# A gather waits for the landing of the third gather ahead instead of the sixth, under a new order

## The chip, the core and the metric

The kernel runs on one core of a Trainium2 chip. Five engines work side by side: TensorE (PE), VectorE (DVE), ScalarE (ACT), GpSimd (POOL) and SyncE (SP); each takes its own instructions in order, and they wait for one another by semaphores. Sixteen DMA engines move data between the chip's memory and the core's buffers. The metric is the device time of one launch in microseconds (us).

## What is computed

The reference adds three things to an input `x` of 2048 rows and 448 columns: `x` itself, a long convolution with gates (A), and a mixture of very many small experts (B). Cut to what matters:

```
xn = layernorm(x)
# A: a 4-tap convolution on k, times v, then a causal convolution of length 2048
#    for each of 448 channels (by Fourier transform), gated by xn
kv  = shift_conv(A_k, A_shift_k) * A_v
y   = irfft(rfft(kv, 4096) * rfft(A_ssm_k, 4096))[:2048] + kv * A_ssm_D
A   = xn * y
# B: 16 heads; each picks 2 of 64*64 experts for each row
q1, q2 = split(xn @ B_w_q)                  # 16 heads, 256 + 256
s1, s2 = q1 @ B_k1.T, q2 @ B_k2.T           # 64 scores each
top two of the sums of the two best of s1 and of s2 -> experts e, weights g = softmax
B   = sum over heads and picks of g * gelu(xn . B_u[e]) * B_v[e]
out = x + A + B
```

For each of the 2048 rows 32 experts are fetched, each a row of `B_u` and a row of `B_v`. In the kernel the two tables lie side by side (`uv`, 896 numbers of 4 bytes for one expert).

## The kernel before, in words

The 2048 rows are 16 tiles `T` of 128. B runs in 128 batches of eight to a tile: batch `b` holds 512 pairs of a row and an expert, and is fetched by four gathers, `r` = 0 to 3. A gather is one indirect DMA that GpSimd issues (line 586): 128 rows of 896 numbers from `uv` into a slot of `ring`, by the list `idx`. The ring holds five batches (`RING`), so the gathers of batch `b` overwrite batch `b - 5`, once its last use is over.

A batch then passes through the engines: VectorE multiplies the four fetched `U` parts by the spread-out rows of xn in one instruction ("prod", line 619); ScalarE sums each of the four parts (line 625) and applies gelu (line 627); GpSimd multiplies by the weights and spreads the coefficients ("co" and "coef", lines 633 and 632; from batch 104 on, `LATE`, VectorE does this); TensorE multiplies the coefficients into the `V` parts and adds up in `pv` ("val", line 638). Around it TensorE makes the scores of later tiles (lines 477 to 481) and the transforms of A (lines 720, 767 and 771, 814, 858 and 865); SP loads A's inputs (`kvh`, line 348, 400 KB each), the Fourier matrices and the query weights.

Nothing of this order is found at run time. A planner in Python (`Plan`) walks through all steps with a cost for each, keeps a clock for each engine and one for the DMA, and lets the ready step with the lowest key go first. A key is the step's due time plus an offset from the table `RANK`: for each group of steps a few knots, between which the offset is interpolated along the group. The order in which the planner starts the steps is the order in which each engine's instructions are written out. In the planner a gather occupies POOL for 0.96, its landing occupies the DMA for `DLAND` = 1.2, and a step on another engine that needs it waits 0.15 and 1.6 more for the two hops.

Two things hold a gather back beside its ring slot and its list. The first is its mark: the last step on PE that ended at least `LEAD` = 0.5 before the gather's start in the plan; on the chip the gather waits for that instruction. The second is the landing of an earlier gather, `OUTSTANDING` places ahead, both in the plan (`after`) and on the chip:

```python
if len(gins) >= OUTSTANDING:
    tc.add_manual_dep(g, gins[-OUTSTANDING], ..., reason="gathers on their way")
...
after = (landed[-OUTSTANDING],) if len(landed) >= OUTSTANDING else ()
i = op("POOL", 0.96, f, r=[("idx", T % 8, j // 2)], w=rk, key=tb(b) - 14.0, after=after, name="gather")
d = op("DMA", DLAND, None, key=tb(b) - 14.0, after=(i,), name="landing")
...
elif o.pace:
    tc.add_manual_dep(i, o.pace.last, ..., reason="gathers keep pace with PE")
```

After some val steps a few small matmuls fill a short planned idle time of PE (line 1094); how many is worked out from the plan.

Of the kernel before, what the change touches and what calls it, by code (L numbers as in the profile page):

```python
# [18 lines left out]
S, D, H, E = 2048, 448, 16, 64  # L19
# [75 lines left out]
class Plan:  # L95
# [13 lines left out]
    def op(self, eng, dur, fn, r=(), w=(), key=0.0, acq=None, rel=None, nb=0.0, name="", after=()):  # L109
        o = Op()  # L110
        o.eng, o.dur, o.fn, o.key, o.acq, o.rel, o.nb, o.name = eng, dur, fn, key, acq, rel, nb, name
        o.deps, o.users, o.start, o.pace, o.last = set(after), [], None, None, None
        o.group = name + self.stage
        for k in r:
            if k in self.writer:
                o.deps.add(self.writer[k])
            self.readers.setdefault(k, []).append(o)
        for k in w:
            if k in self.writer:
                o.deps.add(self.writer[k])  # L120
            o.deps.update(self.readers.get(k, ()))
            self.writer[k] = o
            self.readers[k] = []
        o.deps.discard(o)
        self.ops.append(o)
        return o
# [90 lines left out]
CONV = {"in0": (77.8, 157.8), "sp0": (177.4, 373.1), "out0": (383.1, 393.1),  # L217
        "in1": (388.1, 396.9), "sp1": (396.9, 561.6), "out1": (561.6, 586.6)}
DMA_RATE = 0.421
OUTSTANDING = 6  # L220
LEAD = 0.5
RANK = {
# [6 lines left out]
    "SPlate@out1": (-46.5, -46.5, -46.5, -57.0), "SPwq": (0.0, 0.0, 45.5, 0.0), "SPx": (6.0, 6.0, 19.5, 22.0), "bad": (178.0, 100.0, 62.0, 46.5),  # L229
    "co": (-1740.0, 1197.0, -1227.0, -3082.0), "coef": (-33.5, -40.5, -46.0, 6.0), "ds": (22.0, -93.0, -157.5, -36.0),  # L230
    "es": (79.5, 106.0, 108.5, 109.0), "fin@out0": (-413.0, -296.5, -286.5, 40.5), "fin@out1": (0.5, -32.0, -27.5, -27.5),
    "flag": (-22.5, -47.5, -14.0, -53.0), "fold": (50.0, 36.5, 0.0, 0.0), "gat": (13.0, 13.0, 13.0, 9.0), "gate@out1": (6.5, 14.5, -60.5, -123.0),
    "gateG@out0": (83.0, -13.0, 54.5, 64.0), "gateG@out1": (-81.0, -64.5, -137.5, -144.0), "gather": (2080.5, 2339.0, 2195.5, 3324.0),
    "gelu": (164.5, 57.0, 133.0, 285.5), "hh@sp0": (8.0, -21.0, -25.0, -24.5), "hh@sp1": (123.5, 413.0, 124.0, 164.0),
    "idx": (-94.5, -44.0, 35.5, -83.0), "join": (-75.5, -75.5, -75.0, -66.0), "kv@in0": (-829.5, -476.5, -686.5, -690.5),
    "kv@in1": (85.0, 90.5, 112.5, 143.0), "landing": (36.0, 242.5, 1246.5, -266.5), "late@out1": (87.0, -40.5, -164.0, -260.0),
    "lateD@out1": (344.5, 342.0, 247.0, 196.0), "mi": (-280.5, -150.0, 455.5, 455.5), "mx": (-7077.5, -8642.5, -7977.0, -6331.5),
    "newton": (67.5, 142.0, 224.5, 283.5), "pk": (-14.5, -10.0, -32.0, -8.0), "place": (-628.5, -829.0, -301.5, -212.5),
# [6 lines left out]
    "stats": (1206.5, 960.0, 979.0, 837.5), "store": (43.0, 28.0, 12.5, 7.0), "storeD": (23.5, 22.0, 74.0, 52.5),  # L245
# [3 lines left out]
    "tw@sp1": (-23.5, -160.0, -53.5, -133.5), "val": (87.5, -236.5, 21.0, -42.0), "whi": (495.0, 545.0, 210.5, 67.0),  # L249
# [4 lines left out]
}  # L254
LATE = 104
DLAND = 1.2
# [17 lines left out]
def one_pass(ctx, tc, x, wq, kk, uv, kvh, cst1, cst2, fq, out, flag):  # L274
# [119 lines left out]
    def tb(b):  # L394
        return T0 + PACE * min(b, TURN) + PACE2 * max(b - TURN, 0)
# [177 lines left out]
    def last_val(i, b):  # L573

        tc.declare_no_dep(i, group=GROUP, reason="the last product of the batch, which ends after the others, is waited for")
        if b >= 0:
            tc.add_manual_dep(i, vins[b], mybir.DependencyInfo(mybir.DependencyClass.Sync, mybir.DependencyReason.DATA),
                              reason="the products of the batch that was here have been made")

    def gather(T, j):  # L580
        b = NB * T + j
        for r in range(4):
            dst = ring[:, b % RING, r, :]

            def f(r=r, dst=dst):
                g = nc.gpsimd.indirect_dma_start(dst, None, uv, bass.IndirectOffsetOnAxis(ap=idx[:, T % 8, r, j:j + 1], axis=0)).ins  # L586
                last_val(g, b - RING)
                if len(gins) >= OUTSTANDING:

                    tc.add_manual_dep(g, gins[-OUTSTANDING], mybir.DependencyInfo(mybir.DependencyClass.Sync, mybir.DependencyReason.DATA),  # L590
                                      reason="gathers on their way")
# [3 lines left out]
            rk = [("U", b % RING, r), ("V", b % RING, r)]  # L595
            after = (landed[-OUTSTANDING],) if len(landed) >= OUTSTANDING else ()
            i = op("POOL", 0.96, f, r=[("idx", T % 8, j // 2)], w=rk, key=tb(b) - 14.0, after=after, name="gather")
# [559 lines left out]
```

## Time and profile before

| what | value |
|---|---|
| time, median of 3 runs | 909.22 us (908.57 to 912.37) |
| the profiled execution's own time | 899.54 us |
| its span, first to last instruction | 897.6 us |
| its mean granted TensorE clock | 0.931 |
| busy: PE, DVE, POOL, ACT | 734.1, 673.5, 593.5, 568.2 us |
| moved by DMA | 279.47 MB, 311 GB/s on the mean |
| of it by gathers | 234.91 MB |
| gathers (line 586) | 512, first start 41.6 us, last start 871.5 us |
| POOL busy with gathers | 509.3 us, idle just before them 270.6 us |

The rows of the profile that are shown below are of a few views. The page gives busy times, the span in 40 equal slices (a digit is the busy share in tenths), the DMA queues (q0 holds the gathers, q1 the loads and stores issued by SP), and the chain of work that ended last. A group's row has the line, engine, operation, output and input, count, then busy time and mean ns of one, then the idle time just before and what ended it. A row of waits has who waited, for whom, and the us in total, the times and the longest. A row of the timeline has start, duration, engine, line and operation, and in brackets the idle time before it with what ended it; a row of the chain has start, duration and what. A row of stretches has the bounds and the length, the busy time of PE, PE's weight loads, DVE, ACT and POOL with counts, the granted clock, the DMA share and GB/s.

### The profile page before, as it was taken

To read this page: it belongs to the slowest core of one execution; us is meant where nothing else is said; L and a number is where in the kernel's file an instruction comes from. 1 tells how busy PE (TensorE), PEld (TensorE's weight loads), DVE (VectorE), ACT (ScalarE), POOL (GpSimd) and SP (SyncE) were. 2 spreads that over 40 slices of the span, in tenths; PEclk is the share of its full clock that TensorE was granted. 3 is DMA by queue.
4 is the path that set the end of the run, shared out by engine and by line. 5 is a ranking of instruction groups with operands and counts; after the bars stand their busy time and mean duration, and the time that the engine had idled before them with its cause. 6 is when DMAs were issued, how large, how long until landed. Compare 5 with 4: busy or idle time off the path is not lost.

```text
span 897.6 us, 15165 instructions
## 1 busy us (share of the span) xinstructions
PE 734.1 (82%) x4696; PEld 465.9 (52%) x4696; DVE 673.5 (75%) x1570; ACT 568.2 (63%) x1874; POOL 593.5 (66%) x740
## 2 busy tenths in 40 slices
PE   5988988898888889888797878787688887778776
PEld 2436756556555565556465645465343443345554
DVE  3568988887787878787887867758798897864454
ACT  2598664557565766566663675537798887764562
POOL 0157587886777767776777677757877776665550
PEclk9899999998999989998998989999999999997797
DMA  9898798888989999898889899988999999999885
GB/s 372 345 398 296 229 309 304 294 284 301 313 314 318 304 314 311 309 332 297 297 293 344 294 309 343 356 326 295 354 318 325 319 328 313 309 309 336 299 299 143
DMA packets 62586, 279.47 MB, mean 311 GB/s; under 512 B 14112, under 2 KB 23584, under 8 KB 62240
## 3 DMA queue, kind: packets, MB, share of 16 engines
q0 software_dynamic: 40960, 234.91, 75.2%
q1 hardware_dynamic: 21536, 43.49, 13.7%
q8 instruction: 39, 0.64, 0.3%
q14 instruction: 51, 0.42, 0.1%
HBM read 272.29 MB, written 6.08 MB: 310 GB/s over the span
## 4 chain that ended last, share of the span: by engine, by line
PE 49%; ACT 12%; issue 12%; DVE 9%; DMA 7%; POOL 7%; another core or an unknown queue 3%; DVEq 0%; POOLq 0%; SPq 0%; ACTq 0%
PE pv L638 9%; ACT ring L625 6%; POOL ring L586 5%; PE bank L477 4%; PE bank L720 4%; PE bank L478 3%; PE bank L479 3%; PE bank L814 3%; PE pv L1094 3%; PE bank L771 3%; DMA ring<-in_uv_dram,idx 3%; PE bank L865 2%; DVE ring L619 2%; DMA S<-in_kvh_dram 2%
## 5 line engine op out<-in xcount | busy, mean ns | idle before, releaser
L586 POOL DMA_INDIRECT ring<-in_uv_dram,idx x512 | 509.3, 995 | 270.6 <-issue 91.3
L625 ACT ACTIVATE ring<-ring 128x448 f32<-128x448 f32 x512 | 288.4, 567 | 49.8 <-DVE ring L619 30.5
L619 DVE TENSOR_TENSOR ring<-ring,xs 128x1792 f32<-128x1792 f32 x128 | 256.9, 2014 | 54.7 <-DMA ring<-in_uv_dram,idx 37.6
L638 PE MATMUL pv<-ring,cc 128*32 128x448 f32 x1024 | 136.4, 604 | 67.3 <-issue 36.5
L486 DVE MAX8 SC<-bank 128x8 f32<-128x64 f32 x512 | 118.5, 232 | 37.2 <-PE bank L481 10.0
L625 ACT ACTIVATION_READ_ACCUMULATOR ring<-ring 128x1 f32 x512 | 97.0, 189 | 0.0
L1094 PEld LDWEIGHTS pv<-c 128*128 128x128 f32 x596 | 80.3, 201 | 26.6 <-issue 25.5
L477 PE MATMUL bank<-WR,xh 128*128 128x512 f32 x192 | 84.4, 440 | 2.7 <-ACT R L724 1.0
L720 PE MATMUL bank<-c,S 128*64 128x132 f32 x896 | 68.1, 295 | 22.1 <-issue 7.0
L1094 PE MATMUL pv<-c 128*128 128x64 f32 x596 | 85.6, 285 | 0.0
L478 PE MATMUL bank<-WR,xh 128*128 128x512 f32 x192 | 78.1, 407 | 0.0
L638 PEld LDWEIGHTS pv<-ring,cc 128*32 128x32 f32 x1024 | 21.3, 112 | 108.3 <-issue 65.0
L479 PE MATMUL bank<-WR,xl 128*128 128x512 f32 x192 | 77.3, 403 | 0.0
L720 PEld LDWEIGHTS bank<-c,S 128*64 128x64 f32 x896 | 53.1, 143 | 45.3 <-issue 12.5
L771 PE MATMUL bank<-x1b,S 128*128 128x336 f32 x132 | 51.6, 505 | 10.8 <-DVE x1b L839 7.0
L724 ACT ACTIVATE x1b<-bank 128x264 f32<-128x264 f32 x84 | 30.8, 387 | 40.0 <-PE bank L720 29.7
L788 DVE TENSOR_TENSOR S<-bank,S 128x224 f32<-128x224 f32 (+1 forms) x66 | 40.5, 620 | 18.6 <-ACT S L782 13.4
L703 DVE TENSOR_TENSOR S<-S 128x1024 f32<-128x1024 f32 x28 | 34.9, 1245 | 25.7 <-PE bank L720 11.5
L493 DVE FIND_INDEX8 SC<-SC,bank 128x8 uint32<-128x256 f32 x128 | 52.5, 423 | 0.0
L477 PEld LDWEIGHTS bank<-WR,xh 128*128 128x128 f32 x192 | 37.9, 197 | 26.6 <-issue 11.5
L782 ACT ACTIVATE S<-bank 64x112 f32<-64x112 f32 x132 | 33.9, 257 | 21.8 <-PE bank L767 13.0
L632 POOL TENSOR_TENSOR cc<-sm,c 128x128 f32<-128x128 f32 x104 | 46.0, 442 | 2.2
(142 smaller groups left out, 1090.8 us busy)
## 6 DMA issues: line engine op xcount, KB each, us to landing
R<-in_wq_dram SPq DMA_DIRECT2D x16, 896.0 KB
S<-in_kvh_dram SPq DMA_DIRECT2D x28, 400.0 KB
ring<-in_uv_dram,idx POOLq DMA_INDIRECT x512
S<-in_fq_dram SPq DMA_DIRECT2D x32, 128.0 KB
XA<-in_x_dram SPq DMA_DIRECT2D x2, 1344.0 KB
out_dram<-fo SPq DMA_DIRECT2D x12, 224.0 KB
x1b<-out_dram SPq DMA_DIRECT2D x9, 224.0 KB
out_dram<-XA SPq DMA_DIRECT2D x2, 840.0 KB
```

Source lines behind the costliest of these rows:

```text
L477: nc.tensor.matmul(o, xh[:, c, :], wh[:, c, ns], start=(c == 0), stop=False)
L478: nc.tensor.matmul(o, xh[:, c, :], wl[:, c, ns], start=False, stop=False)
L479: nc.tensor.matmul(o, xl[:, c, :], wh[:, c, ns], start=False, stop=False)
L486: nc.vector.max(mx[:, 8 * n + j, :] if safe else m2[:, m, 2 * j:2 * j + 8], bank[s.i][:, 64 * j:64 * j + 64])
L493: nc.vector.max_index(m4i[:, 2 * m + g, :], m2[:, m, 8 * g:8 * g + 8], bank[s.i][:, 256 * g:256 * g + 256])
L586: g = nc.gpsimd.indirect_dma_start(dst, None, uv, bass.IndirectOffsetOnAxis(ap=idx[:, T % 8, r, j:j + 1], axis=0)).ins
L619: op("DVE", dve(m * D), lambda: nc.vector.tensor_mul(U[:, :m, :], U[:, :m, :], xs[:, :m, :D]), r=["xs"], w=u[:m], key=k, name="prod")
L625: op("ACT", 0.575, lambda r=r: nc.scalar.activation(U[:, r, :], U[:, r, :], AF.Copy, accum_out=aw[:, r:r + 1]), w=[u[r], ("aw", b % 4, r)] ...
L638: v = nc.tensor.matmul(pv[32 * r:32 * r + 32, :D], cc[b % 3][:, r, :], ring[:, b % RING, r, D:], start=(j == 0), stop=(j == NB - 1), tile_ ...
L720: nc.tensor.matmul(o[64 * i:64 * i + 64, w * j:w * j + w], src, f1[:, i, :], start=True, stop=True, tile_position=(0, 64 * i))
L771: op("PE", 0.95 * n / 448 + 0.05, lambda t=t, sl=sl: nc.tensor.matmul(bank[sl.i][:, :n], fm, x1[p][:, :, q, t, :], start=True, stop=True), ...
L1094: nc.tensor.matmul(pv[:, D:], ident, c1[:, P:P + 512 - D], start=False, stop=False)
```

## The change

`OUTSTANDING` goes from 6 to 3, so that a gather waits, beside its mark, for the landing of the third gather ahead of it, in the plan and on the chip. The offsets in `RANK` are replaced throughout by ones searched under that limit; each group now has seven knots where it had four, and the group "gate@out0", which had no offset, has one. Nothing else differs: the same steps, planner, costs, `LEAD`, `RING` and due times. Since the order follows from the offsets, every engine's instructions may stand in another order, and the marks, the issues of loads on SP and the filling matmuls may move with it.

```diff
-OUTSTANDING = 6
+OUTSTANDING = 3
 LEAD = 0.5
 RANK = {
-    "DMAc1": (-1.0, 0.0, 8.0, 64.5), "DMAc2": (43.5, 4.0, 37.0, 128.5), "DMAfb@out1": (247.5, -85.5, 210.0, 115.5),
...
-    "gateG@out0": (83.0, -13.0, 54.5, 64.0), "gateG@out1": (-81.0, -64.5, -137.5, -144.0), "gather": (2080.5, 2339.0, 2195.5, 3324.0),
...
+    "DMAc1": (-0.5, 60.0, -4.0, 62.0, 66.0, 88.5, 101.0), "DMAc2": (9.5, -29.0, -37.0, -37.5, -25.5, -32.5, 50.5),
...
+    "gate@out0": (-119.5, -124.5, -110.5, -54.5, -104.0, 5.0, -21.0), "gate@out1": (93.0, 111.0, 62.0, 76.5, 97.5, 44.0, 22.5),
+    "gateG@out0": (-34.0, 21.5, -6.0, -6.0, -4.0, -9.0, -35.0), "gateG@out1": (52.0, 66.5, 99.5, 120.5, 75.0, 42.5, 14.0),
+    "gather": (2662.0, 2607.5, 2615.5, 2445.5, 2351.0, 2680.5, 3398.5), "gelu": (170.0, 120.5, 81.5, 118.5, 162.5, 259.0, 378.0),
...
```

More of the change, by code (lines that the diff above doesn't have):

```diff
@@ L219 @@
 DMA_RATE = 0.421
-OUTSTANDING = 6
+OUTSTANDING = 3
 LEAD = 0.5
 RANK = {
[6 rows of a table removed]
[L229 to L232, printed above, removed]
-    "gateG@out0": (83.0, -13.0, 54.5, 64.0), "gateG@out1": (-81.0, -64.5, -137.5, -144.0), "gather": (2080.5, 2339.0, 2195.5, 3324.0),
[L234 to L238, printed above, removed]
[6 rows of a table removed]
-    "stats": (1206.5, 960.0, 979.0, 837.5), "store": (43.0, 28.0, 12.5, 7.0), "storeD": (23.5, 22.0, 74.0, 52.5),
[3 rows of a table removed]
-    "tw@sp1": (-23.5, -160.0, -53.5, -133.5), "val": (87.5, -236.5, 21.0, -42.0), "whi": (495.0, 545.0, 210.5, 67.0),
[4 rows of a table removed]
[4 rows of a table added]
+    "DMAwq": (-21.5, -19.5, 33.0, -42.5, -89.5, -48.5, 1.0), "DMAx": (-285.0, -148.5, -33.5, 30.5, 52.0, 31.5, -17.5),
[5 rows of a table added]
+    "SPwq": (-14.0, -14.0, -14.0, -13.0, 18.5, -13.0, -4.5), "SPx": (-18.5, -21.0, -21.0, -35.0, -31.0, -14.0, 54.5),
[4 rows of a table added]
+    "fold": (-108.5, -170.5, -136.5, -130.0, -183.0, -187.0, -161.0), "gat": (73.5, 9.5, 30.0, 42.5, 53.0, 173.5, -3.0),
+    "gate@out0": (-119.5, -124.5, -110.5, -54.5, -104.0, 5.0, -21.0), "gate@out1": (93.0, 111.0, 62.0, 76.5, 97.5, 44.0, 22.5),
+    "gateG@out0": (-34.0, 21.5, -6.0, -6.0, -4.0, -9.0, -35.0), "gateG@out1": (52.0, 66.5, 99.5, 120.5, 75.0, 42.5, 14.0),
+    "gather": (2662.0, 2607.5, 2615.5, 2445.5, 2351.0, 2680.5, 3398.5), "gelu": (170.0, 120.5, 81.5, 118.5, 162.5, 259.0, 378.0),
+    "hh@sp0": (-2.0, 38.0, 37.0, 10.0, 10.5, -10.0, -9.0), "hh@sp1": (40.0, 410.5, 385.5, 224.0, 224.5, 217.5, 316.5),
+    "idx": (-458.0, -374.0, -360.5, -370.5, -241.0, -306.5, -364.0), "join": (10.5, 10.5, 10.5, 0.0, 21.5, 10.5, 6.5),
[14 rows of a table added]
+    "spread": (-336.0, -148.5, 25.0, -176.0, -279.0, -123.0, 116.0), "stats": (1255.5, 1039.0, 915.5, 925.0, 934.5, 817.5, 776.5),
+    "store": (-76.5, -136.0, -134.5, -128.0, -206.0, -104.5, -102.0), "storeD": (-6.0, 24.5, -5.5, -15.0, -2.0, 7.5, 75.0),
[5 rows of a table added]
+    "val": (101.5, -42.5, -220.5, -40.0, 50.0, 45.5, -17.0), "whi": (113.5, 207.5, 262.0, 53.5, -97.5, -120.5, -277.5),
[6 rows of a table added]
```

55 rows, old and new, of the table RANK are left out of this document.

## The prediction

> **What bounds the kernel now.** I read the page first, its engine shares, the 40 slices and the DMA queues, then the chain, then the groups and waits of GpSimd, then single stretches of the timeline, because the change concerns one kind of instruction only.
>
> ```profile
> PE 734.1 (82%) x4696; PEld 465.9 (52%) x4696; DVE 673.5 (75%) x1570; ACT 568.2 (63%) x1874; POOL 593.5 (66%) x740
> ...
> DMA  9898798888989999898889899988999999999885
> ...
> q0 software_dynamic: 40960, 234.91, 75.2%
> q1 hardware_dynamic: 21536, 43.49, 13.7%
> ...
> PE 49%; ACT 12%; issue 12%; DVE 9%; DMA 7%; POOL 7%; another core or an unknown queue 3%; DVEq 0%; POOLq 0%; SPq 0%; ACTq 0%
> ...
> L586 POOL DMA_INDIRECT ring<-in_uv_dram,idx x512 | 509.3, 995 | 270.6 <-issue 91.3
> ```
>
> No engine is full. The chain of work that ended last lies on PE for half of its length and changes hands all the time. What is almost full is the transfer side: the DMA row stands at 8 or 9 tenths in nearly every slice, and the gathers' queue (q0) alone takes 75.2% of 16 engines, so a gather costs 0.752 x 897.6 / 512 = 1.32 us of all engines together, and q1's traffic adds 0.137 x 897.6 / 512 = 0.24 us to each. The gathers are therefore a second stream beside PE, and its speed matters.
>
> ```profile
> L586 POOL DMA_INDIRECT ring<-in_uv_dram,idx x512: 943/951/1939, 41.6 to 871.5; - x171
> ...
> L586 POOL DMA_INDIRECT ring<-in_uv_dram,idx x64 | 63.4, 990 | 20.3 <-issue 11.6 <-PE bank L771 6.1 <-remote 1.2
> ...
> 640.00:735.00 95.00, 79.24 (x354) 37.21 (x354) 82.49 (x101) 82.58 (x248) 74.15 (x98) 0.96 0.93 322
> ```
>
> The first row (the answer on the gather's line) says that 512 gathers start within 871.5 - 41.6 = 829.9 us, one every 1.62 us. The other two are the densest stretch, 640 to 735 us: 64 gathers in 95 us, one every 1.48 us. GpSimd's groups there name what ended the idle time before the gathers: its own issue and a mark on PE (L771), no landing. So today the limit of six is not what paces them; the marks and the issue are.
>
> **The change, part by part.** It moves one wait and it re-orders. No instruction is added to any engine: 512 gathers, 128 products, the same coefficients, the same loads.
>
> *The wait.* What matters is how long a gather takes from its start to the moment at which a waiting engine gets going. Three places show it, since there a product on VectorE (line 619) waited for the last gather of its batch. Of each, the gathers before it, and then the product:
>
> ```profile
> 123.70 0.96 POOL L586 DMA_INDIRECT ring<-in_uv_dram,idx  x1 [0.16 <-issue]
> ...
> 125.58 1.13 POOL L586 DMA_INDIRECT ring<-in_uv_dram,idx  x1 [0.16 <-issue]
> 127.02 0.95 POOL L586 DMA_INDIRECT ring<-in_uv_dram,idx  x1 [0.30 <-issue]
> ...
> 128.36 0.96 POOL L586 DMA_INDIRECT ring<-in_uv_dram,idx  x1 [0.15 <-issue]
> ...
> 129.91 0.99 POOL L586 DMA_INDIRECT ring<-in_uv_dram,idx  x1 [0.16 <-issue]
> ...
> 136.09 2.02 DVE L619 TENSOR_TENSOR ring<-ring,xs 128x1792 f32<-128x1792 f32 x1 [1.74 <-DMA ring<-in_uv_dram,idx]
> ```
>
> ```profile
> 700.56 1.17 POOL L586 DMA_INDIRECT ring<-in_uv_dram,idx  x1 [1.01 <-PE bank L771]
> ...
> 702.12 0.96 POOL L586 DMA_INDIRECT ring<-in_uv_dram,idx  x1 [0.15 <-issue]
> 703.09 0.42 POOL L632 TENSOR_TENSOR cc<-sm,c 128x128 f32<-128x128 f32 x1
> 703.67 0.99 POOL L586 DMA_INDIRECT ring<-in_uv_dram,idx  x1 [0.16 <-issue]
> 704.96 0.95 POOL L586 DMA_INDIRECT ring<-in_uv_dram,idx  x1 [0.30 <-issue]
> ...
> 705.94 2.02 DVE L619 TENSOR_TENSOR ring<-ring,xs 128x1792 f32<-128x1792 f32 x1 [1.17 <-DMA ring<-in_uv_dram,idx]
> ```
>
> ```profile
> 867.96 0.95 POOL L586 DMA_INDIRECT ring<-in_uv_dram,idx  x1 [0.30 <-issue]
> 871.52 0.95 POOL L586 DMA_INDIRECT ring<-in_uv_dram,idx  x1 [2.61 <-ACT S L860]
> ...
> 876.15 2.02 DVE L619 TENSOR_TENSOR ring<-ring,xs 128x1792 f32<-128x1792 f32 x1 [3.62 <-DMA ring<-in_uv_dram,idx]
> ```
>
> From start to release: 136.09 - 129.91 = 6.18 us behind a tight row of gathers; 705.94 - 700.56 = 5.38 us in the dense stretch; 876.15 - 871.52 = 4.63 us for the very last gather, which left 3.56 us behind the one before it. The second fence shows the new wait at work by hand: the gather at 704.96 is the third after the one at 700.56, whose release is seen at 705.94. Under the limit it would start about 1.0 us later, and the one behind it would in turn wait for the gather of 702.12.
>
> Under the change gather i cannot start before gather i-3 is released, so three gathers fill one such time: the stream can do no better than a gather per 4.63 / 3 = 1.54 us, 5.38 / 3 = 1.79 us, or 6.18 / 3 = 2.06 us. Against that stand 1.62 us on the average and 1.48 us in the dense stretch, where 5.38 / 1.48 = 3.6 gathers are under way at a time. So by the trace the limit of three lies right at the speed that the kernel needs, while the limit of six (5.38 / 6 = 0.90 us) lies below the spacing that GpSimd's own work allows (703.67 to 704.96 to 706.21, about 1.25 us).
>
> Which value? With three at most, fewer gathers queue ahead than in the dense stretch, so 5.38 us is too long; but two others are nearly always under way, which the gather of 871.52 did not have, so 4.63 us is too short. I take the middle, 5.0 us, a gather per 1.67 us: 512 x 1.67 = 855 us for the stream against 829.9, that is +25 us. At the ends: 512 x 1.54 = 788 us, no loss on the average and only 64 x (1.54 - 1.48) = 4 us in the dense stretch; 512 x 1.79 = 916 us, +87 us. I count the whole of the +25, because the stream has hardly a cover: the products wait for landings already (21 times, 37.6 us, in the row below), and PE's val matmuls (line 638) run in a written order behind them. Early batches have some lead over their products, which can swallow a late gather or two but not a stream that is slower throughout.
>
> The Trainium skill, page "DMA: Bandwidth & Descriptors", section "Anatomy of one DMA — SWDGE (gpsimd) path", speaks against this forecast: it gives a fit of about 2.0 us and the bytes at 436 GB/s for a transfer issued by GpSimd. By that page a gather (234.91 MB / 512 = 0.459 MB) would be an estimated 3.05 us, 4.0 us with its issue, or 1.33 us per gather with three under way, and the limit would cost nothing. The 4.63 and 5.38 us of this trace disagree with it; they were taken with other transfers running.
>
> *What is queued behind the waiting gather.* GpSimd also makes the coefficients of 104 batches (lines 632, 633), in order with the gathers, and PE waits for them:
>
> ```profile
> DVE ring L619 <- DMA ring<-in_uv_dram,idx: 37.6, 21, 4.1
> ...
> PEld pv L638 <- POOL cc L632: 34.0, 26, 2.9
> ...
> PE pv L638 <- POOL cc L632: 25.0, 22, 2.5
> ```
>
> Those are 48 waits and 59 us. A gather that stands 1.67 - 1.25 = 0.42 us longer than its shortest spacing delays a coefficient behind it by as much: at most 48 x 0.42 = 20 us, if every one of these waits still ends last. I take zero, because it is the same pause of GpSimd, already counted in the stream, and keep the 20 us for the upper end.
>
> *The other queues.* The loads on SP are moved by the new order too. Three of them stand on the chain:
>
> ```profile
> 477.51 6.96 DMA S<-in_kvh_dram
> ...
> 593.37 5.64 DMA S<-in_kvh_dram
> ...
> 623.57 6.78 DMA S<-in_kvh_dram
> ```
>
> They share the 16 engines with the gathers. If a shallower queue brought all to the shortest of them, it would give (6.96 - 5.64) + (6.78 - 5.64) = 2.5 us; below nothing, if they are issued later in the new order. I take zero. The same skill page, section "Queues, rings and completion order", says that an engine takes turns between its queues packet by packet; by that a load on SP would not wait behind all gathers that are under way, and the depth would matter little to it. No row here separates the two.
>
> *The new order.* Nothing in the trace of before shows it. Its planner holds a landing for 0.96 + 0.15 + 1.2 + 1.6 = 3.91 us from start to release (the gather's own duration, the two hops, DLAND), so under three it can plan a gather per 1.30 us, where the rows above say 1.54 to 1.79. The order is thus searched for a stream that the chip won't give, and it cannot raise that stream. Where it helps is in moving gathers to places with room. Below, it could take back at most the 37.6 us of VectorE's waits; above, it could cost the 20 us named. I take zero.
>
> *The sum.* 899.5 us (the profiled execution; span 897.6) + 25 = 924.5 us. The median shown, 909.2, lies 9.7 us above that execution, so the forecast for the median is 934 us.
>
> **The rivals.**
> 1. *The limit is hidden.* With fewer under way the transfer falls to 4.6 us, and 1.54 us per gather is enough. For it: the last gather's 4.63 us, and GpSimd idle for 270.6 us before gathers. Against it: two others are under way in a full stream, and the DMA row stands at 8 or 9 tenths even where the gathers are one per 1.62 us. It gives 909 + 0 to 4 us. The fit of the Trainium skill's page "DMA: Bandwidth & Descriptors", above, would make this rival the likeliest.
> 2. *Faster, by the same mechanism from the other side.* Even spacing takes away the bunches: the gather of 129.91 took 6.18 us since it left behind four others within 6.2 us. If such ones came down to 5 us, the products would get back a part of their 37.6 us; a third is 12.5 us, with the loads' 2.5 us 15 us, and 894 us. It decides as soon as a gather's time falls below 3 x 1.62 = 4.86 us, since then the stream has room and only the gain is left. Against it: those 37.6 us stand at 21 places, 4.1 us at most, and the same products would now wait for gathers that start later.
> 3. *Dearer.* The time doesn't fall at all: 1.79 us per gather, 909 + 87 = 996 us. For it: the 0.24 us of q1's traffic stays whatever the depth. Against it: fewer gathers must queue less.
>
> **How the numbers follow.** My forecast, a stream of 1.64 to 1.72 us per gather with its coefficients (918 to 958 us): 0.49. Rival 3: 0.13. Rival 1: 0.13. Rival 2, with a better order as another way to the same sign: 0.25. A change within 0.5% (4.5 us) is what this measurement can't tell from none. So slower 0.62, same 0.13, faster 0.25. The range leaves out half of rival 3 and a good part of rival 2's tail: 893 to 980 us.
>
> **What would show it.** Right: in GpSimd's waits the landing of a gather (DMA ring) becomes a large releaser of the gather, tens of us where the page of before has almost none; the dense stretch thins to about 57 gathers in 95 us (one per 1.67); from a gather's start to the product that it releases it takes about 5.0 us; the DMA row falls by a tenth in places; VectorE's wait for landings grows above 37.6 us. Wrong: gathers still one per 1.5 us in the dense stretch, or releases within 4.6 us, or GpSimd's waits ended by marks on PE as now; then the limit rarely binds and the order decides. If the chain's PE share rises and the span falls, rival 2 holds.

## The result: slower by about a fifth, and the profile after

The changed kernel takes 1075.66 us (median of 4 runs, 1072.58 to 1078.19) against 908.89 us for the kernel before: a ratio of 1.189, 95% interval 1.183 to 1.195, taken from the fast runs (the two medians alone give 1.183). The forecast had the sign and a loop of three gathers as the mechanism, 934 us, and a range up to 980 us; the loss is 167 us instead of 25.

The page of the changed kernel answers line by line to the one of before (shares and counts as there):

```profile
PE 830.9 (77%) x4844; PEld 536.7 (50%) x4844; DVE 675.4 (63%) x1570; ACT 574.7 (53%) x1874; POOL 580.8 (54%) x740
...
DMA  9987767778788888878788888788887787878786
...
q0 software_dynamic: 40960, 234.91, 69.0%
q1 hardware_dynamic: 21536, 43.49, 11.4%
...
DMA 38%; PE 27%; issue 12%; POOL 10%; DVE 10%; ACT 2%; DVEq 0%; POOLq 0%; SPq 0%; ACTq 0%
...
L604 POOL DMA_INDIRECT ring<-in_uv_dram,idx x512 | 497.2, 971 | 466.9 <-DMA ring<-in_uv_dram,idx 142.5
```

Read the chain first: DMA has gone from 7% to 38% of it, PE from 49% to 27%. The gathers' own instructions (now line 604) are no longer than before; what has grown is GpSimd's idle time ahead of them, from 270.6 to 466.9 us, with a landing as the largest releaser. The DMA row has fallen by one or two tenths in 26 of its 40 slices: the transfers have room, and the kernel waits for them all the same.

The gathers' line gives the whole loss in one row (durations in ns, then first and last start):

```profile
L604 POOL DMA_INDIRECT ring<-in_uv_dram,idx x512: 940/946/1971, 39.1 to 1056.7; - x171
```

From first to last gather 1017.6 us pass, 829.9 before: +187.7 us, of which the span shows 1076.1 - 897.6 = +178.5, since the ends around the stream got 9 us shorter. A gather starts every 1.99 us. Who waits for the stream is in the waits (total us, times, longest):

```profile
DVE ring L637 <- DMA ring<-in_uv_dram,idx: 225.4, 74, 6.6
ACT ring L643 <- DVE ring L637: 197.1, 73, 9.2
PEld pv L656 <- POOL cc L650: 153.5, 71, 6.4
POOL ring L604 <- DMA ring<-in_uv_dram,idx: 142.5, 114, 3.8
...
PE pv L656 <- POOL cc L650: 127.6, 58, 6.2
```

Product, sums, coefficients: each step of a batch now stands behind the landing.

Why 1.99 us? A stretch of GpSimd's timeline in the changed kernel (start, duration, in brackets the idle time before) and the chain through the same stretch:

```profile
370.39 0.94 POOL L604 DMA_INDIRECT ring<-in_uv_dram,idx  x1 [1.03 <-PE bank L832]
372.18 0.94 POOL L604 DMA_INDIRECT ring<-in_uv_dram,idx  x1 [0.84 <-PE pv L656]
373.88 0.94 POOL L604 DMA_INDIRECT ring<-in_uv_dram,idx  x1 [0.76 <-issue]
375.64 0.94 POOL L604 DMA_INDIRECT ring<-in_uv_dram,idx  x1 [0.81 <-DMA ring<-in_uv_dram,idx]
377.74 0.95 POOL L604 DMA_INDIRECT ring<-in_uv_dram,idx  x1 [1.15 <-DMA ring<-in_uv_dram,idx]
379.99 0.95 POOL L604 DMA_INDIRECT ring<-in_uv_dram,idx  x1 [1.31 <-DMA ring<-in_uv_dram,idx]
```

```profile
370.39 5.00 DMA ring<-in_uv_dram,idx
375.38 0.26 issue
375.64 5.04 DMA ring<-in_uv_dram,idx
380.68 0.03 issue
380.71 0.05 DVEq L637
380.76 0.04 issue
380.81 2.02 DVE ring L637
```

The fourth gather is the third after the first: 375.64 - 370.39 = 5.25 us for three. The next two loops are 377.74 - 372.18 = 5.56 and 379.99 - 373.88 = 6.11 us; over all 512 it is 3 x 1.99 = 5.97 us. The second view splits the first of these loops: 5.00 us until the landing, 0.26 us until the waiting gather starts. That is the good case. The chain some 35 us later has the other:

```profile
410.76 0.02 POOLq L604
410.77 0.72 issue
411.50 5.24 DMA ring<-in_uv_dram,idx
```

Here a gather has two waits, and one of them stands on an instruction of its own in GpSimd's queue (POOLq). When that one ends last, 0.72 us more pass before the gather starts. The packet records of q0 (80 to a gather, the last 16 of them of 4 bytes) give the averages: 4.64 us from a gather's start to the end of its last packet, 1.35 us from there to the start of the gather that waits for it, which is called the restart below. The semaphore tells of a landing some 0.35 us behind the last packet (the median of the 256 gathers for which the old order under the same wait, the first experiment below, has all the events), so 1.35 us is about 1.0 us behind the landing.

The same records show that most gathers start close behind the landing, far more often than the rows name it: 68% of the gathers start within 1.3 us of the last packet of the third gather ahead, and 91% within 2 us; in the kernel before, 1% start within 2 us of that of the sixth. And the restart is not the price of a wait alone. In 290 of the 509 loops GpSimd had not yet ended the instruction ahead, mostly a gather or a coefficient, when the landing came (put at 0.35 us behind the last packet); there the restart is 1.50 us on the average, in the others 1.15 us.

### The profile page after: what moved, and what is told of

Its sections match the earlier page's. It is cut to its first block, busy times and chain, and to the rows that moved or that the text cites. A ratio compares the mean times of both kernels' runs of the same rounds, so it can differ in the third digit from the quotient of the medians.

```text
span 1076.1 us, 15472 instructions
## 1 busy us (share of the span) xinstructions
PE 830.9 (77%) x4844; PEld 536.7 (50%) x4844; DVE 675.4 (63%) x1570; ACT 574.7 (53%) x1874; POOL 580.8 (54%) x740
## 4 chain that ended last, share of the span: by engine, by line
DMA 38%; PE 27%; issue 12%; POOL 10%; DVE 10%; ACT 2%; DVEq 0%; POOLq 0%; SPq 0%; ACTq 0%
DMA ring<-in_uv_dram,idx 38%; POOL ring L604 7%; PE pv L656 6%; DVE ring L637 4%; PE pv L1112 3%; PE bank L738 2%; PE bank L495 2%; DVE SC L504 2%; PE bank L497 2%; POOL cc L650 2%; PE bank L496 2%; ACT ring L643 2%; PE bank L433 1%; PE bank L789 1%; PE bank L834 1%
## 5 line engine op out<-in xcount | busy, mean ns | idle before, releaser
L604 POOL DMA_INDIRECT ring<-in_uv_dram,idx x512 | 497.2, 971 | 466.9 <-DMA ring<-in_uv_dram,idx 142.5
L637 DVE TENSOR_TENSOR ring<-ring,xs 128x1792 f32<-128x1792 f32 x128 | 257.8, 2016 | 230.7 <-DMA ring<-in_uv_dram,idx 225.4
L656 PE MATMUL pv<-ring,cc 128*32 128x448 f32 x1024 | 155.8, 687 | 164.8 <-POOL cc L650 127.6
L1112 PEld LDWEIGHTS pv<-c 128*128 128x128 f32 x744 | 117.8, 236 | 40.5 <-issue 39.1
L656 PEld LDWEIGHTS pv<-ring,cc 128*32 128x32 f32 x1024 | 22.2, 119 | 209.3 <-POOL cc L650 153.5
L1112 PE MATMUL pv<-c 128*128 128x64 f32 x744 | 123.4, 320 | 0.0
L738 PE MATMUL bank<-c,S 128*64 128x132 f32 x896 | 80.3, 339 | 23.1 <-ACT ring L643 10.9
L495 PE MATMUL bank<-WR,xh 128*128 128x512 f32 x192 | 85.8, 447 | 3.3 <-DVE S L806 1.1
L738 PEld LDWEIGHTS bank<-c,S 128*64 128x64 f32 x896 | 66.0, 170 | 42.7 <-ACT ring L643 15.2
L496 PE MATMUL bank<-WR,xh 128*128 128x512 f32 x192 | 79.1, 412 | 0.0
L650 POOL TENSOR_TENSOR cc<-sm,c 128x128 f32<-128x128 f32 x104 | 46.1, 443 | 5.4
L789 PEld LDWEIGHTS bank<-x1b,S 128*128 128x128 f32 x132 | 26.0, 218 | 41.6 <-DVE S L806 12.1
```

What stands on the lines that cost most here:

```text
L495: nc.tensor.matmul(o, xh[:, c, :], wh[:, c, ns], start=(c == 0), stop=False)
L496: nc.tensor.matmul(o, xh[:, c, :], wl[:, c, ns], start=False, stop=False)
L637: op("DVE", dve(m * D), lambda: nc.vector.tensor_mul(U[:, :m, :], U[:, :m, :], xs[:, :m, :D]), r=["xs"], w=u[:m], key=k, name="prod")
L650: last_val(ve.tensor_mul(cc[b % 3], co[:, :, None].broadcast_to([P, 4, 32]), rep[:, None, :].broadcast_to([P, 4, 32])).ins, b - 3)
L656: v = nc.tensor.matmul(pv[32 * r:32 * r + 32, :D], cc[b % 3][:, r, :], ring[:, b % RING, r, D:], start=(j == 0), stop=(j == NB - 1), tile_ ...
L738: nc.tensor.matmul(o[64 * i:64 * i + 64, w * j:w * j + w], src, f1[:, i, :], start=True, stop=True, tile_position=(0, 64 * i))
```

## The experiments

In all of them `OUTSTANDING` in the plan stays as it was in the kernel named, so order and fill are those of that kernel, and its marks too where they are not said to be left out. Where the wait on the chip is another, it has a number of its own:

```diff
+WAIT = 3
...
-                if len(gins) >= OUTSTANDING:
-                    tc.add_manual_dep(g, gins[-OUTSTANDING], ...)
+                if len(gins) >= WAIT:
+                    tc.add_manual_dep(g, gins[-WAIT], ...)
```

The experiments ran in three groups, each on another chip. The kernel before took 847.43 us in the first, 894.97 in the second and 845.86 in the third, so each ratio is against the kernel before of its own group.

**Wait and order apart (first group).** The old order with the wait for the third:

> The order, the plan and the marks of before; only the wait on the chip is for the third gather ahead. Theory A (the wait alone: a gather per 1.99 us as in the changed kernel, since 4.64 us from start to landing and 1.35 us from landing to the start of the gather that waits make 5.98 us for three): 1050 to 1090 us, first to last gather about 1000 us. Rival B (the new order is what costs, since it was searched for a gather per 1.30 us): at most 990 us. My own prediction's term (1.67 us per gather) would give 934 us.

Measured: 1076.3 us, ratio 1.274 (1.261 to 1.287). The new order with the wait for the sixth (`WAIT = 6`):

> The order, the plan and the marks of the changed kernel; only the wait on the chip is for the sixth gather ahead again. Theory A: the order is near neutral, 895 to 925 us, and the clock that PE is granted comes back to about 0.93 by itself. Rival B: 980 us or more. Rival C (order and wait work on each other: the order suffers only under the wait): 895 to 925 us here, and below 1050 us in the run with the old order and the wait for the third.

Measured: 892.63 us, ratio 1.051 (1.036 to 1.065). The wait alone does all of it, and rivals B and C are out: the old order under the new wait takes the same 1076 us as the changed kernel. But the order is not neutral either: by itself it costs 5.1%, which was not expected. Under the wait for the third nothing of that shows. The two streams, old order first:

```profile
L587 POOL DMA_INDIRECT ring<-in_uv_dram,idx x512: 940/947/1959, 41.5 to 1052.8; - x171
```

```profile
L605 POOL DMA_INDIRECT ring<-in_uv_dram,idx x512: 941/949/1926, 39.1 to 872.3; - x171
...
DVE ring L638 <- DMA ring<-in_uv_dram,idx: 115.7, 57, 5.1
```

That is a gather per 1.98 us, and per 1.63 us with the wait back at six.

**Other depths.** The old order with the wait for the fourth, then the new one:

> The order of before, the wait on the chip for the fourth gather ahead. Theory A: with four in the same loop of about 4.9 + 1.35 = 6.25 us a gather per 1.56 us is possible, below the 1.62 us of before, so only dense stretches lose: 905 to 930 us. If instead every wait for a landing costs by itself, whatever the depth: above 950 us.

> The order of the changed kernel, the wait on the chip for the fourth gather ahead. Theory A: 900 to 935 us, within 10 us of the run with the old order and the wait for the fourth. Rival B: 980 us or more.

Measured: 933.16 us (1.105, 1.094 to 1.116) and 936.63 us (1.110, 1.099 to 1.121). Both lie a little above the expected range, since four gathers took 6.78 us (below) and not the 6.25 us assumed. And the loss of 86 and 89 us is not small: the kernel before is faster on this chip than the 909 us from which the range was drawn. That the two orders agree again, though they differ by 5% under the wait for the sixth, says once more that the loop sets the end. The fifth, in the second group:

> The order of before, the wait for the fifth gather ahead. Theory A: five in a loop of 5.1 + 1.35 = 6.5 us would allow a gather per 1.30 us, near GpSimd's own 1.25 us, so the wait hardly ever ends last: within 15 us of the kernel before. If each wait for a landing costs by itself: half of the loss with the fourth, some 40 us or more.

Measured: 903.05 us (1.008, 1.004 to 1.011), as theory A had it; a wait for a landing doesn't cost by itself. The second, in the third group:

> The order of before, the wait for the second gather ahead. Theory A: start to landing about 4.4 us (one other under way) and 1.35 us from landing to the next start, 5.75 us for two, a gather per 2.88 us, 511 x 2.88 = 1470 us from first to last, 1520 to 1560 us in all. If the time from start to landing falls in proportion to the depth: below 1300 us.

Measured: 1382.78 us (1.633, 1.625 to 1.641), between the two expectations. The stream of the fourth, the fifth and the second, in that order:

```profile
L587 POOL DMA_INDIRECT ring<-in_uv_dram,idx x512: 941/949/1865, 40.6 to 906.9; - x171
```

```profile
L587 POOL DMA_INDIRECT ring<-in_uv_dram,idx x512: 940/947/2022, 41.3 to 875.0; - x171
```

```profile
L587 POOL DMA_INDIRECT ring<-in_uv_dram,idx x512: 940/947/1982, 42.1 to 1355.2; - x171
...
POOL ring L587 <- DMA ring<-in_uv_dram,idx: 406.8, 290, 5.8
```

Divided by 511 these are 1.70, 1.63 and 2.57 us per gather. Times the depth, the loop is 5.14 us at two, 5.94 at three, 6.78 at four; at five (8.2) it no longer binds. By the packet records the time from start to last packet is 4.06, 4.64 and 5.00 us at two, three and four, and the restart 1.08, 1.30 and 1.78 us. At four the landing mostly comes before it is the gather's turn: in 457 of 508 loops GpSimd had not yet ended the instruction ahead, against 287 of 509 at three and 42 of 510 at two. The 1.70 us per gather at four are thus set by GpSimd's own work as well as by the wait. My expectation for two took the restart of three, and counted the 0.35 us from the last packet to the landing twice: the medians from start to landing, the last number of these two rows of DMA issues, are 4.2 us at two and 4.9 us at three (the latter from the changed kernel in the next experiment).

```profile
ring<-in_uv_dram,idx POOLq DMA_INDIRECT x512, 4.2
```

```profile
ring<-in_uv_dram,idx POOLq DMA_INDIRECT x512, 4.9
```

So the transfer does get shorter with fewer under way, but by 0.4 to 0.6 us for each gather less, while the loop loses a whole gather.

The Trainium skill, page "DMA: Bandwidth & Descriptors", section "Anatomy of one DMA — SWDGE (gpsimd) path", gives the fit from which the prediction estimated 4.0 us with the issue. At a depth of two the 4.2 us from start to landing are near it; at three, 4.9 us, they no longer are.

**The whole on one more chip.** The changed kernel in the third group:

> The changed kernel once more, beside the others of this group on one chip. Theory A (a loop of fixed times, three gathers in 5.98 us, sets the end): 1070 to 1080 us whatever the kernel before takes on this chip (847 to 909 us so far), as the old order under the same wait took 1076 us. If PE's clock or the chip's transfer speed sets it: the time moves with that of the kernel before.

Measured: 1074.98 us, ratio 1.269 (1.262 to 1.275). The medians of the kernel before lie up to 63 us apart between groups, those of the changed one 1 us: a stream bound by this loop doesn't use what a chip has to spare. What it is that a chip has to spare was not found.

**The restart.** The marks left out of the changed kernel:

```diff
-            elif o.pace:
+            elif o.pace and o.name != 'gather':
```

> The changed kernel with the marks on PE left out; a gather then waits for the third gather's landing, its ring slot and its list alone. Theory A1 (where a gather has two waits the landing is put on an instruction of its own ahead of the gather, and 0.72 us pass from the end of that one to the gather's start; with one wait the gather itself waits and starts at once): the loop shortens by about 0.5 us in most cases, 5.98 to about 5.45 us, a gather per 1.82 us, 985 to 1010 us. Rival A2 (0.72 us is what GpSimd needs to start a gather after any wait for a landing): 1060 to 1080 us.

Measured: 1052.84 us (1.177, 1.170 to 1.184), where the changed kernel took 1075 us in its own groups: about 22 us less, where 65 to 90 were expected. The waits on their own instruction fell from the first of these rows to the second (the changed kernel's, then this one's):

```profile
L604 POOLq EVENT_SEMAPHORE  x431: 17/17/1397, 48.6 to 1055.3; - x144
```

```profile
L604 POOL DMA_INDIRECT ring<-in_uv_dram,idx x512: 943/949/1943, 39.5 to 1028.1; - x171
L604 POOLq EVENT_SEMAPHORE  x181: 17/43/43, 57.8 to 1026.7; - x181
```

The loop shortened only from 5.97 to 5.80 us. 181 gathers still have a second wait, for their list or ring slot, and in 252 of the 509 loops GpSimd was still on the instruction ahead when the landing came, so that a quicker start after a wait had less to gain there. A1's direction is right (the marks do cost time beside the landing), its size was too large. Then a memset in front of each gather, to take the wait for the landing off it:

```diff
+                if len(gins) >= OUTSTANDING:
+                    c = nc.gpsimd.memset(sm[:, 60:61], 0.0).ins
+                    tc.add_manual_dep(c, gins[-OUTSTANDING], ...)
                 g = nc.gpsimd.indirect_dma_start(...)
```

> The changed kernel; a memset of one column on GpSimd ahead of each gather takes the wait for the landing, the gather keeps its mark. A1: the memset starts at once and the gather about 0.15 us behind it, so that 0.72 us becomes about 0.3 us, the loop about 5.6 us, a gather per 1.86 us, 1000 to 1040 us; the memsets' own time (some 0.2 us each) lies inside the wait. A2: 1060 us or more.

Measured: 1087.85 us (1.215, 1.208 to 1.222), no gain. The timeline of GpSimd shows why, after a wait and without one:

```profile
407.65 0.10 POOL L605 MEMSET sm<- 128x1 f32 x1 [1.02 <-DMA ring<-in_uv_dram,idx]
408.33 0.94 POOL L608 DMA_INDIRECT ring<-in_uv_dram,idx  x1 [0.59 <-DVE SC L504]
...
411.18 0.10 POOL L605 MEMSET sm<- 128x1 f32 x1
411.42 0.98 POOL L608 DMA_INDIRECT ring<-in_uv_dram,idx  x1
```

From the end of a memset that had waited to the gather 0.58 us pass, from one that had not, 0.14 us. Over the whole trace, where the gather is the next instruction, the median is 0.59 us behind the 155 memsets that waited for a landing (90% of them between 0.59 and 0.61) and 0.20 us behind the 261 that waited for nothing. So whatever waits ahead of the gather, the gather starts late behind it; only a gather that does the waiting itself starts soon. A1, which blamed the separate instruction alone, falls in this form, and A2 does as well, because of the 0.26 us above. What GpSimd does in that half microsecond stays open.

**The order's own cost.** The kernel before again, for its profile on the second chip:

> The kernel before once more, for its profile on the chip of these runs, where it takes 847 us instead of 909. All theories: a gather per 1.5 to 1.55 us. If the two chips differ in the gathers' time from start to landing, it is below 5 us in the dense stretch here; if they differ in the clock that PE is granted, it is above 0.94.

Measured: 890.57 us in one run; a gather per 1.61 us, a clock of 0.922. That chip is near the one of the first result, so why the other two run this kernel in 846 and 847 us was not settled. Its wait of VectorE for landings is 36.2 us, against the 115.7 us of the new order above, which ran on another chip:

```profile
DVE ring L619 <- DMA ring<-in_uv_dram,idx: 36.2, 24, 3.3
```

The new order without its marks, under the wait for the sixth, and the old one without its marks, both in the third group:

> The order of the changed kernel, the wait for the sixth, the marks on PE left out. Theory O1 (what the new order costs under the wait for the sixth, 5.1%, comes from marks that let the gathers start too late: they start 9.4 us behind the release of their ring slot on the median where the old order has 5.0 to 5.5, and VectorE waits 115.7 us for landings instead of 36.2): within 2% of the kernel before, VectorE's waits for landings below 70 us. Theory O2 (the sequence of the steps itself costs it): 4% or more above the kernel before.

> The kernel before without its marks on PE. If marks only delay gathers: 1 to 3% faster. If they keep the queue short and GpSimd's coefficients in time: up to 3% slower, with more than the sixth under way never possible. No theory of the wait for the third gather hangs on it; it is the other half of the run without marks in the new order.

Measured: 859.3 us (1.013, 1.008 to 1.019) and 838.23 us (0.988, 0.982 to 0.994).

```profile
L605 POOL DMA_INDIRECT ring<-in_uv_dram,idx x512: 940/947/1999, 40.8 to 839.7; - x171
...
DVE ring L638 <- DMA ring<-in_uv_dram,idx: 85.6, 46, 4.2
```

```profile
L586 POOL DMA_INDIRECT ring<-in_uv_dram,idx x512: 940/949/1949, 41.5 to 813.2; - x171
...
DVE ring L619 <- DMA ring<-in_uv_dram,idx: 40.3, 29, 4.0
```

Time as O1 had it, VectorE's waits above its 70 us. Without marks the new order is 1.013 / 0.988 = 1.026 times the old one, with them, on the first group's chip, 1.051: roughly half of its cost goes with the marks and the rest is in the sequence, though two chips and the intervals leave that split rough. The last kernel, the old order with the sixth and no marks, is the fastest of all: 1.2% ahead of the kernel before, as expected if marks only delay gathers.

## Why the prediction was wrong, point by point

- *What bounds the kernel, and that the sixth never binds:* right. With the fifth the kernel loses 0.8%.
- *A loop of three gathers sets the speed of the stream:* right, and shown by the depths two and three; at four GpSimd's own work has a part in it.
- *The size of the loop* ("I take the middle, 5.0 us, a gather per 1.67 us"): this is the step that failed. The time to the landing was near it (5.00 and 5.04 us in the chain above, a median of 4.9 us in the changed kernel on the third group's chip). But I read the loop's end from the start of VectorE's product, which came 0.13 us behind the landing in that chain, and the loop closes on GpSimd, where the next gather starts about 1.0 us behind it on the average (1.35 us behind the last packet). The sum had no term for that. The loop was 5.97 us, a gather 1.99 us, the stream +188 us instead of +25. Even my upper end, 1.79 us, left that term out, since all three rows that bounded it ended on the same other engine. The 2.06 us of the tight row, which I did not carry into the sum, lies near the 1.99 us only by coincidence: there it is the transfer that is long (6.06 us to the landing in the chain of before).
- *The coefficients at zero beside the stream:* PE's waits for them grew from 59 us to 153.5 us of its weight loads and 127.6 us of its matmuls, but the stream's +187.7 us already exceeds the span's +178.5, so nothing is left for them outside it. They do have a part in the restart, as GpSimd makes them in order with the gathers, but hardly by waiting: in the whole changed kernel GpSimd stood idle before their two instructions for 2.7 and 5.4 us, and was busy with them for 23.1 and 46.1 us.
- *The loads on SP at zero:* not tried by itself. In the changed kernel's chain the only such load among the longest pieces is that of query weights at its very start (4.91 us).
- *The new order at zero:* wrong when taken alone (+5.1% under the wait for the sixth), without effect here, since the loop hides it.
- *The rivals:* the dearer one was nearest, and it too stopped at 996 us; its reason, that the transfer doesn't get shorter, was not the cause (start to last packet is 5.13 us in the kernel before, 4.64 us in the changed one). The even spacing and the hidden limit would both have needed a loop below 4.9 us.
- *What would show it:* the landing as a releaser of tens of us (142.5), VectorE's waits above 37.6 (225.4), the DMA row a tenth lower, and about 5 us from a gather's start to the product that it releases (380.81 - 375.64 = 5.17 us in the chain above) all came; a gather per 1.67 us in the dense stretch did not.

## What to carry to other kernels

A limit on transfers under way is a loop: it lets through as many transfers as its depth in the time of one whole round, which is issue, transfer, landing, and the restart of the engine that waits, with whatever else that engine has to do first. Take each part from the engine on which it happens; a consumer elsewhere that starts 0.1 us after a landing says nothing about the issuer. Before lowering a depth, multiply the wanted spacing by it and compare with one round, with room to spare. With 1.62 us wanted, three leave 4.86 us for a round of 5.97 us. Four leave 6.48 us for one of about 6.15 us (an estimate: 5.00 us to the last packet and 1.15 us, the median restart at three), and the kernel still lost 10%, on a chip on which it had been faster and so probably wanted less than 1.62 us; the rounds vary, too. Five leave 8.1 us, and the loss was 0.8%, on the chip with 1.61 us.

## What the runs showed of the hardware that was not expected

A gather that waits for a landing itself starts 0.26 us after it in the chain; behind an instruction that waited it starts 0.58 to 0.72 us after that one's end, where the median behind a memset that did not wait is 0.20 us.

The clock that TensorE was granted in the profiled executions went down with the depth: 0.939 and 0.948 under the sixth without marks, 0.912 to 0.931 with waits for the fifth and the sixth, 0.891 to 0.907 for the fourth, 0.826 to 0.854 for the third, 0.738 for the second. In the changed kernel PE was busy for 830.9 us, 734.1 before, 148 more of the small filling matmuls included. Whether the slower clock adds to the time under the wait for the third, or only fills time that PE would spend waiting, was not tried.
